# Attention and MLP backward for one token: all DMAs off GpSimd's queue, and the last head in another order

## Chip, cores and metric

The kernel runs on 1 core of a Trainium2 chip. The metric is the device time in microseconds, the median of several executions.

## The reference

One decode token goes through an attention block with a cache (A) and a Mish MLP (B), mixed by a gate; the result and the gradients for the token, both caches, all weights and the gate are wanted.

```python
def _A_ref(x, k_cache, v_cache, wq, wo):          # H=32 heads, Sk=4096, Dh=128, D=640
    q = (x @ wq).reshape(B, Sq, H, Dh).transpose(0, 2, 1, 3)
    scores = einsum("bhqd,bhkd->bhqk", q, k_cache) * (Dh ** -0.5)
    p = softmax(scores)
    o = einsum("bhqk,bhkd->bhqd", p, v_cache)
    return o.transpose(0, 2, 1, 3).reshape(B, Sq, H * Dh) @ wo

def _B_ref(x, w1, b1, w2):                        # F=1728
    h = einsum("bsd,df->bsf", x, w1) + b1
    act = h * tanh(softplus(h))
    return einsum("bsf,fd->bsd", act, w2)

g = sigmoid((x * gate_w).sum(-1, keepdims=True))
out = g * _A_ref(A_x, ...) + (1 - g) * _B_ref(B_x, ...)
# outputs: out, and its gradients by A_x, k_cache, v_cache, wq, wo, w1, b1, w2, gate_w
```

Everything is bf16. Each head reads K and V (1 MB each) and writes dK and dV (1 MB each): 128 MB of the 165 MB that are moved.

## The kernel before

**Tiles.** K and V of a head are [128, 32, 128]: partition p holds 32 consecutive rows, 8 KB of them. The 32 heads come in 8 groups of G = 4. A group has its 512 columns of wq as `wq_g` [128, 5, 512] (rows of 1,024 bytes in memory) and its rows of wo as `wo_g` [128, 4, 640] (rows of 1,280 bytes), 640 KB each, in rings of three. Their gradients dwq and dwo are written over them in place and stored from there. K has four buffers, V three, the outgoing `o_sb` tiles of dK and dV four. w1, w2 and their gradients live in `w1_sb` and `w2_sb`, 2.2 MB each.

**A head (loop at L581).** TensorE transposes V (`v_tr`) in four blocks of 8, each copied from PSUM by ScalarE (`tr_block`, L406 and L407). `softmax` takes the scores that were made a head earlier; `dP` multiplies the transposed V with the gradient of o; `zd_mm` sums over partitions; `probs` makes p and ds on VectorE. `dv_out` and `dk_out` are outer products on VectorE (L469, two halves), stored by SP (L480, L482). `k_tr` and `scores` prepare the next head, `dq_o` (L492) sums dq and o from K, V, ds and p, and then SP issues the loads of K for head h + 4 and V for head h + 3. dK of a head is made in the next head, except for the last.

**A group.** `g_do`, `g_qcol`, `g_q` and others prepare the next group's q and do rows from its wq and wo. After a group, `f_diag` and `f_bc` broadcast its dq; `f_aT_pe` multiplies o with wo (TensorE); `f_dx` multiplies wq with the broadcast dq on VectorE and sums along the row (the gradient of x); `f_dwq` (VectorE) and `f_dwo` (ScalarE) write the weight gradients; `f_dwq_st` and `f_dwo_st` store them. These run in the heads hh = 0 and hh = 1 of the next group.

**The MLP** is cut into pieces, taken by `mlp_some` and `dw2_some` at the end of each head as far as a budget goes. `m_h` makes a piece of h on one partition and a small DMA carries it over to 32 partitions; two such rows are in use at a time. By head 28 all pieces are done, and dw1 and dw2 are stored (L676 to L681). An engine takes its instructions in the written order, but GpSimd has so few that it runs ahead and issues these stores as soon as their data is there.

**Queues.** SP issues K, V, dK, dV, the MLP's weights, and wq and wo of groups 1 and 2. GpSimd (POOL) issues the other wq and wo loads (L131, L132, L654, L655), b1 (L149), the h rows (L308), dwq and dwo (L278, L284), dw1 and dw2 (L677 to L680) and one small result (L725). A queue's instructions wait in order: one that waits for a semaphore holds back all that stand behind it.

**The end (from L683).** For the last head, groups of its work are done for three heads inside the loop and for the fourth after it; then aT, dx and the gate's gradient are put together, transposed and stored.

Of the kernel before, what the change touches and what calls it, by code (L numbers as in the profile page):

```python
# [16 lines left out]
def kernel(  # L17
# [96 lines left out]
    def load_wq(g, eng):  # L114
        wqs[g] = wts.tile([P, RC, GD], BF16, name="wq_g", tag="wq_g")
        eng.dma_start(wqs[g][:], wq_v[:, :, g * GD:(g + 1) * GD])
# [11 lines left out]
    kts[0] = kv_in.tile([P, J, Dh], BF16, name="Kn", tag="Kn")  # L128
    for c in range(2):
        nc.sync.dma_start(kts[0][:, c * JH:(c + 1) * JH, :], Kv[0][:, c * JH:(c + 1) * JH, :])  # L130
    load_wq(0, nc.gpsimd)  # L131
    load_wo(0, nc.gpsimd)  # L132
    load_v(0)
    load_k(1)
    load_v(1)
# [10 lines left out]
    nc.sync.dma_start(w2_sb[0:FT, FR, :], B_w2[FM:F, :])  # L146
    b1_sb = const.tile([P, FCN], BF16, name="b1_sb")
    nc.vector.memset(b1_sb[:], 0.0)
    nc.gpsimd.dma_start(b1_sb[:, 0:FR], b1_v)  # L149
    nc.gpsimd.dma_start(b1_sb[0:FT, FR:FCN], b1_t)  # L150

    ident_bf = const.tile([P, P], BF16, name="ident_bf")
    nc.gpsimd.memset(ident_bf[:], 0.0)
# [111 lines left out]
    def f_dx(g, c, a=0, b=G, slot=None):  # L265
# [4 lines left out]
        nc.vector.scalar_tensor_tensor(junk[:, cs], in0=wqs[g][:, c, cs], scalar=1.0, in1=gp["dq_bc"][:, cs],  # L270
                                       op0=ALU.mult, op1=ALU.mult, accum_out=dx_parts[:, c, slot:slot + 1])

    def f_dwq(g, c, a=0, b=G):
        cs = slice(a * Dh, b * Dh)
        nc.vector.tensor_scalar(wqs[g][:, c, cs], groups[g]["dq_bc"][:, cs], x_col_f[:, c:c + 1], None, ALU.mult)  # L275

    def f_dwq_st(g):
        nc.gpsimd.dma_start(dwq_v[:, :, g * GD:(g + 1) * GD], wqs.pop(g)[:])  # L278

    def f_dwo(g, hh):  # L280
        nc.scalar.activation(wos[g][:, hh, :], da_bc[:], ACT.Copy, scale=groups[g]["dqo"][:, 1, hh:hh + 1])  # L281

    def f_dwo_st(g, a=0, b=G):
        nc.gpsimd.dma_start(dwo_v[:, g * G + a:g * G + b, :], wos[g][:, a:b, :])  # L284

    h_sb = const.tile([P, FCN], F32, name="h_sb")
    u_sb = const.tile([P, FCN], F32, name="u_sb")
# [11 lines left out]
    def m_h(i):  # L299
        n = FW if i < 4 else FT  # L300
        ps = grp([1, FW], F32, "h_ps")
        for rc in range(RC):
            nc.tensor.matmul(ps[:, 0:n], lhsT=x_col_bf[:, rc:rc + 1], rhs=w1_sb[:, rc, i * FW:i * FW + n],
                             start=(rc == 0), stop=(rc == RC - 1))
        row = dh_bc[0:1, :].bitcast(F32)[:, (i % 2) * FW:(i % 2) * FW + n]
        nc.scalar.copy(row, ps[:, 0:n])
        if i < 4:
            nc.gpsimd.dma_start(h_sb[i * P // 4:(i + 1) * P // 4, 0:FR], row)  # L308
        else:
            nc.gpsimd.dma_start(h_sb[0:FT, FR:FCN], row)  # L310

    def m_np(fc):
        return P if fc < FR else FT
# [264 lines left out]
    g_q(0)  # L578
    g_qs(0)

    for h in range(H):  # L581
        g, hh = h // G, h % G
        nx, pv, last = g + 1 < NG, g > 0, h == H - 1
        v_tr(h, 0)
        v_tr(h, 1)
        mx = softmax(h)
        if h > 0:
            dk_out(h - 1)
        if last:
            f_new(g)  # L590
            f_diag(g, 0, 3)
        if hh == 0 and pv:
            g_dobc(g)
        v_tr(h, 2)
        v_tr(h, 3)
        dP(h)
        if hh == 0 and pv:
            f_bc(g - 1)
            f_aT_pe(g - 1)
        if last:  # L600
            f_bc(g, 0, 3)
            f_aT_pe(g, 0, 3)
        k_tr(h + 1, 0)
        k_tr(h + 1, 1)
        zd_mm(h, mx)
        if hh == 0 and pv:
            f_dx(g - 1, 0)
        if hh == 1 and pv:
            f_dx(g - 1, 3)
        if hh == 2 and nx:  # L610
            g_do(g + 1, 0)
        if hh == 3 and nx:
            g_do(g + 1, 3)
        probs(h, mx)
        k_tr(h + 1, 2)
        k_tr(h + 1, 3)
        dv_out(h)
        scores(h + 1)
        od = dq_o(h)
        load_k(h + KBUFS)  # L620
        load_v(h + VBUFS)
        if last:
            dk_out(h)
        dqo_red(h, od)
        budget = 0.0
        if last:
            for i in range(3):
                f_dwo(g, i)
            f_dwo_st(g, 0, 3)
            for c in range(RC):  # L630
                f_dx(g, c, 0, 3)
            for c in range(RC):
                f_dwq(g, c, 0, 3)
        if hh == 0:
            if nx:
                g_new(g + 1)
            if pv:
                f_aT_add(g - 1)
                f_dx(g - 1, 1)
                f_dx(g - 1, 2)  # L640
                f_dwo(g - 1, 0)
                f_dwo(g - 1, 1)
            budget = 2.7
        if hh == 1:
            if pv:
                f_dx(g - 1, 4)
                for c in range(RC):
                    f_dwq(g - 1, c)
                f_dwq_st(g - 1)
                f_dwo(g - 1, 2)  # L650
                f_dwo(g - 1, 3)
                f_dwo_st(g - 1)
            if g + 2 < NG:
                load_wq(g + 2, nc.gpsimd if pv else nc.sync)  # L654
                load_wo(g + 2, nc.gpsimd if pv else nc.sync)  # L655
            budget = 1.8
        if hh == 2:
            if nx:
                g_do(g + 1, 1)
                g_do(g + 1, 2)  # L660
                g_qcol(g + 1)
            budget = 2.7
        if hh == 3:
            if nx:
                g_docol(g + 1)
                g_dodiag(g + 1)
                g_q(g + 1)
                g_qs(g + 1)
                f_new(g)
                f_diag(g)  # L670
            budget = 1.8
        if h >= 2:
            mlp_some(budget)
            dw2_some(2)
        if h == H - 4:
            assert not mq and dw2_next[0] == FCN  # L676
            nc.gpsimd.dma_start(dw1_v, w1_sb[:])  # L677
            for a, b in W2P:
                nc.gpsimd.dma_start(dw2_v[:, a:b, :], w2_sb[:, a:b, :])
            nc.gpsimd.dma_start(out_8[FM:F, :], w2_sb[0:FT, FR, :])  # L680
            nc.sync.dma_start(db1_row, dh_bc[0:1, :])  # L681

    g = NG - 1  # L683
    f_diag(g, 3, 4)
    f_aT_add(g)
    f_bc(g, 3, 4)
    f_aT_pe(g, 3, 4)
    f_dwo(g, 3)
    f_dwo_st(g, 3, 4)
    for c in range(RC):  # L690
        f_dx(g, c, 3, 4, NG)
    for c in range(RC):
        f_dwq(g, c, 3, 4)
    f_dwq_st(g)
    f_aT_add(g)

    fin = const.tile([P, 3 * RC], F32, name="fin")
    gb = const.tile([P, RC], F32, name="gb")
    nc.vector.tensor_scalar(gb[:], bT[:], omg_all[:], None, ALU.mult)
    nc.vector.scalar_tensor_tensor(fin[:, 0:RC], in0=aT_acc[:], scalar=g_all[:], in1=gb[:], op0=ALU.mult, op1=ALU.add)  # L700
    amb = const.tile([P, RC], F32, name="amb")
    nc.vector.tensor_tensor(amb[:], aT_acc[:], bT[:], ALU.subtract)
# [3 lines left out]
                                   accum_out=dgp[:])  # L706
    dg_ps = grp([P, 1], F32, "dg_ps")
    nc.tensor.matmul(dg_ps[:], lhsT=ones_f[:], rhs=dgp[:], start=True, stop=True)
    gg = const.tile([P, 1], F32, name="gg")
    nc.vector.tensor_tensor(gg[:], g_all[:], omg_all[:], ALU.mult)  # L710
    dz = const.tile([P, 1], F32, name="dz")
    nc.vector.tensor_tensor(dz[:], dg_ps[:], gg[:], ALU.mult)
    nc.vector.tensor_scalar(fin[:, 2 * RC:3 * RC], x_col_f, dz[:], None, ALU.mult)
    dxs = const.tile([P, RC], F32, name="dxs")
    nc.vector.reduce_sum(dxs[:], dx_parts[:], axis=AX.X)
# [6 lines left out]
    fin_rows = const.tile([3 * RC, P], BF16, name="fin_rows")  # L722
    nc.scalar.copy(fin_rows[:], fin_ps[:])
    nc.scalar.dma_start(out0_rows, fin_rows[0:RC, :])
    nc.gpsimd.dma_start(out1_rows, fin_rows[RC:2 * RC, :])  # L725
    nc.sync.dma_start(out9_rows, fin_rows[2 * RC:3 * RC, :])


# [28 lines left out]
```

## Time and profile before

| | us |
|---|---|
| median of 3 runs | 419.07 (418.73 to 420.15) |
| profiled execution, its own time | 423.44 |
| its span, first to last instruction | 421.7 |
| TensorE busy | 318.5 (76%) |
| VectorE busy | 307.6 (73%) |
| ScalarE busy | 212.8 (50%) |
| GpSimd busy | 38.1 (9%) |

A page of the profile has the busy time of each engine, the span in 40 slices of 10.5 us (busy tenths, the granted TensorE clock, the busy share of the 16 DMA engines and the GB/s they moved), the DMA queues, the chain of work that ended last, the costliest groups of instructions, and the DMA issues with the time to their landing. PE is TensorE, DVE VectorE, ACT ScalarE, POOL GpSimd; L406 is line 406. Two groups and four kinds of issue that matter here:

```profile
L469 DVE TENSOR_TENSOR o_sb<-qs_row,ds 128x2048 bf16<-128x2048 bf16 x64 | 78.1, 1260 | 6.4 <-DMA out_dram<-o_sb 6.4
...
L270 DVE SCALAR_TENSOR_TENSOR junk<-wq_g,dq_bc 128x512 bf16<-128x512 bf16 (+2 forms) x45 | 27.1, 627 | 4.4 <-ACT dq_bc L233 4.4
...
out_dram<-wq_g POOLq DMA_DIRECT2D x8, 640.0 KB, 10.5
out_dram<-wo_g POOLq DMA_DIRECT2D x7, 640.0 KB, 14.1
wq_g<-in_A_wq_dram POOLq DMA_DIRECT2D x6, 640.0 KB, 11.8
wo_g<-in_A_wo_dram POOLq DMA_DIRECT2D x6, 640.0 KB, 12.2
```

The trace behind the page can be asked for any stretch: the instructions in order of time with what ended the wait before them, the chain of waits, the landing of each DMA, and sums by window.

### The profile page before, as it was taken

The numbers are of one execution on the slowest core, as the hardware profiler recorded it, in microseconds if no ns is written. First come the engines' busy times: TensorE is split into PE (matmuls) and PEld (weight loads), VectorE is DVE, ScalarE is ACT, GpSimd is POOL, SyncE is SP. The second block draws the span as 40 slices with busy tenths as digits, with TensorE's granted clock in tenths as the row PEclk, the third lists the DMA queues.
The fourth block names the chain that finished last, engine by engine and source line by source line (L and its number), as shares of the span: only waits on it lengthen the run. The fifth ranks groups of instructions, "written<-read, shape, count | busy, mean of one in ns | idle before, by whom it ended". The sixth has DMA issues, their size and how long they took to land.

```text
span 421.7 us, 15327 instructions
## 1 busy us (share of the span) xinstructions
PE 318.5 (76%) x6749; PEld 288.9 (69%) x6757; DVE 307.6 (73%) x837; ACT 212.8 (50%) x439; POOL 38.1 (9%) x61
## 2 busy tenths in 40 slices
PE   1598949878689779877987797877778888657621
PEld 1487928778679778767877686876768776647620
DVE  0536735788859987799979788689887975728683
ACT  2255425674346544655577765655346644436321
POOL 5000010001100100001104100001100310001001
PEclk9999888999699898898997989688898998869955
DMA  8999999999999999999999999999999999999783
GB/s 301 390 410 421 422 399 416 392 364 410 412 400 393 378 421 404 423 420 380 418 401 424 419 420 408 420 401 368 418 396 411 390 419 409 415 421 390 308 332 112
DMA packets 28073, 165.05 MB, mean 391 GB/s; under 512 B 3092, under 2 KB 5461, under 8 KB 12006
## 3 DMA queue, kind: packets, MB, share of 16 engines
q1 hardware_dynamic: 22412, 141.28, 83.0%
q0 software_dynamic: 5552, 22.79, 13.7%
q8 instruction: 53, 0.87, 0.8%
q14 instruction: 14, 0.11, 0.1%
q10 hardware_dynamic: 42, 0.01, 0.0%
HBM read 82.03 MB, written 82.03 MB: 389 GB/s over the span
## 4 chain that ended last, share of the span: by engine, by line
PE 33%; issue 21%; ACT 19%; DVE 17%; DMA 6%; POOL 1%; POOLq 0%; ACTq 0%; DVEq 0%
PE tr L406 14%; PE od L492 9%; ACT VT L407 8%; ACT KT L407 6%; DMA wo_g<-in_A_wo_dram 3%; DVE o_sb L469 3%; PE S L412 3%; DVE junk L366 2%; PE DP L412 2%; DVE junk L219 2%; PE q_ps L197 2%; DVE mjunk L388 2%; ACT e_bf L443 2%; DMA out_dram<-o_sb 2%; DMA h_sb<-dh_bc 2%
## 5 line engine op out<-in xcount | busy, mean ns | idle before, releaser
L406 PE MATMUL tr<-ident_bf,Vn 128*128 128x128 bf16 x1024 | 76.6, 232 | 28.7 <-ACT VT L407 18.6
L407 ACT COPY KT<-tr 128x512 f32<-128x512 f32 x128 | 70.7, 587 | 50.9 <-PE tr L406 50.7
L406 PEld LDWEIGHTS <-Vn 128*128 128x128 bf16 x1024 | 68.4, 105 | 38.7 <-issue 28.5
L406 PE MATMUL tr<-ident_bf,Kn 128*128 128x128 bf16 x1024 | 84.5, 247 | 7.7 <-DMA Kn<-in_A_k_cache_dram 5.0
L406 PEld LDWEIGHTS <-Kn 128*128 128x128 bf16 x1024 | 77.7, 115 | 9.8 <-DMA Kn<-in_A_k_cache_dram 5.0
L469 DVE TENSOR_TENSOR o_sb<-qs_row,ds 128x2048 bf16<-128x2048 bf16 x64 | 78.1, 1260 | 6.4 <-DMA out_dram<-o_sb 6.4
L407 ACT COPY VT<-tr 128x512 f32<-128x512 f32 x128 | 69.1, 586 | 22.3 <-PE tr L406 21.9
L469 DVE TENSOR_TENSOR o_sb<-do_row,p 128x2048 bf16<-128x2048 bf16 x64 | 75.2, 1217 | 1.2 <-DMA out_dram<-o_sb 1.2
L412 PE MATMUL DP<-doz,VT 128*128 128x32 bf16 x1024 | 39.6, 179 | 24.9 <-ACT VT L407 21.5
L412 PEld LDWEIGHTS <-VT 128*128 128x128 bf16 x1024 | 33.0, 97 | 29.9 <-ACT VT L407 29.4
L412 PE MATMUL S<-qz,KT 128*128 128x32 bf16 x1024 | 37.1, 180 | 3.0 <-ACT KT L407 0.4
L434 ACT ACTIVATE dgm<-ident_bf,m 128x128 f32<-128x128 bf16 x32 | 12.8, 402 | 50.8 <-DVE m L432 50.8
L412 PEld LDWEIGHTS <-KT 128*128 128x128 bf16 x1024 | 32.5, 98 | 6.3 <-ACT KT L407 5.5
L492 PE MATMUL od<-p,Vn 128*128 128x32 bf16 x1024 | 31.6, 177 | 3.9 <-issue 3.9
L492 PE MATMUL od<-ds,Kn 128*128 128x32 bf16 x1024 | 31.2, 178 | 2.6 <-issue 1.5
L492 PEld LDWEIGHTS <-Vn 128*128 128x128 bf16 x1024 | 28.5, 96 | 4.4 <-issue 4.4
L492 PEld LDWEIGHTS <-Kn 128*128 128x128 bf16 x1024 | 28.7, 97 | 2.8 <-issue 2.8
L270 DVE SCALAR_TENSOR_TENSOR junk<-wq_g,dq_bc 128x512 bf16<-128x512 bf16 (+2 forms) x45 | 27.1, 627 | 4.4 <-ACT dq_bc L233 4.4
L219 DVE SCALAR_TENSOR_TENSOR junk<-wo_g,da_bc 128x640 bf16<-128x640 bf16 x32 | 25.4, 819 | 0.4 <-DMA wo_g<-in_A_wo_dram 0.4
L278 POOL DMA_DIRECT2D out_dram<-wq_g x8 | 7.1, 884 | 206.3 <-DVE wq_g L275 106.2
L281 ACT ACTIVATE wo_g<-da_bc,dqo 128x640 bf16<-128x640 bf16 x32 | 24.5, 814 | 0.0
L440 DVE TENSOR_REDUCE negM<-mx 128x1 f32<-128x128 f32 x32 | 9.2, 286 | 20.2 <-PE mx L438 20.2
(146 smaller groups left out, 319.4 us busy)
## 6 DMA issues: line engine op xcount, KB each, us to landing
out_dram<-o_sb SPq DMA_DIRECT2D x62, 1024.0 KB, 12.2
Vn<-in_A_v_cache_dram SPq DMA_DIRECT2D x32, 1024.0 KB, 14.8
Kn<-in_A_k_cache_dram SPq DMA_DIRECT2D x31, 1024.0 KB, 15.2
out_dram<-wq_g POOLq DMA_DIRECT2D x8, 640.0 KB, 10.5
out_dram<-wo_g POOLq DMA_DIRECT2D x7, 640.0 KB, 14.1
wq_g<-in_A_wq_dram POOLq DMA_DIRECT2D x6, 640.0 KB, 11.8
wo_g<-in_A_wo_dram POOLq DMA_DIRECT2D x6, 640.0 KB, 12.2
w_sb<-in_B_w_dram SPq DMA_DIRECT2D x1, 2160.0 KB, 17.1
```

The source lines that it names most:

```text
L197: nc.tensor.matmul(ps[:], lhsT=x_col_bf[:, rc:rc + 1].to_broadcast([P, P]), rhs=wqs[g][:, rc, :], start=(rc == 0), stop=(rc == RC - 1))
L219: nc.vector.scalar_tensor_tensor(junk[:], in0=wos[g][:, hh, :], scalar=1.0, in1=da_bc[:], op0=ALU.mult, op1=ALU.mult, accum_out=gp["do_col ...
L270: nc.vector.scalar_tensor_tensor(junk[:, cs], in0=wqs[g][:, c, cs], scalar=1.0, in1=gp["dq_bc"][:, cs], op0=ALU.mult, op1=ALU.mult, accum_ ...
L281: nc.scalar.activation(wos[g][:, hh, :], da_bc[:], ACT.Copy, scale=groups[g]["dqo"][:, 1, hh:hh + 1])
L366: nc.vector.scalar_tensor_tensor(junk[0:n, :], in0=w2_sb[0:n, fc, :], scalar=dm[0:n, fc:fc + 1], in1=db_bc[0:n, :], op0=ALU.mult, op1=ALU. ...
L406: nc.tensor.transpose(tp[:, t, :], src[:, c * TB + t, :], ident_bf[:])
L407: nc.scalar.copy(dst[:, sl, :].rearrange("p a b -> p (a b)").bitcast(F32), tp[:].rearrange("p a b -> p (a b)").bitcast(F32))
L412: nc.tensor.matmul(out, lhsT=T[:, j, :], rhs=zrow[:, J - 1 - j:2 * J - 1 - j], start=(j == 0), stop=(j == J - 1))
L434: nc.scalar.activation(dgms[h][:], ident_bf[:], ACT.Copy, scale=m32[:])
L440: nc.vector.tensor_reduce(negM[:], mx[:, 0:P], axis=AX.X, op=ALU.max, negate=True)
L469: nc.vector.tensor_tensor(dst[:, a:b, :].rearrange("p j (k t) -> p j k t", t=4), row.rearrange("p (k t) -> p k t", t=4).unsqueeze(1).to_br ...
L492: nc.tensor.matmul(out, lhsT=N[:, j, :], rhs=c4[:, 4 * j:4 * j + W], start=(j == 0), stop=(j == J - 1))
```

## The change

Three things change.

- **Queues.** wq and wo of group 0, b1, the h rows and all dwo stores are issued by ScalarE; the later wq and wo loads and the dwq stores by SP; the MLP's gradients by SP, dw2 at the end of head 28 and dw1 at the end of head 29, behind the last V load. GpSimd issues no DMA.
- **Places in the loop.** A group's dwq store stands at the end of head hh = 2 (before: hh = 1), the load of wq and wo two groups ahead at the end of hh = 3 (before: hh = 1).
- **The last head** leaves the loop and is written out. Its wq group is transposed (20 blocks, `wq_tr`), into a free K buffer, and `l_pe` makes both aT and dx of the last group by TensorE, for three heads first and then for the fourth; `f_dx` is not used there. `l_dwq` makes the fourth head's dwq on ScalarE. dK of head 30 comes after `probs` of head 31, and dV and dK of head 31 come last, after the sums of the small results.

```diff
-    load_wq(0, nc.gpsimd)
-    load_wo(0, nc.gpsimd)
+    load_wq(0, nc.scalar)
+    load_wo(0, nc.scalar)
...
-    nc.gpsimd.dma_start(b1_sb[:, 0:FR], b1_v)
+    nc.scalar.dma_start(b1_sb[:, 0:FR], b1_v)
...
+    def wq_tr(k):
+        if k == 0:
+            wqT[0] = kv_in.tile([P, J, Dh], BF16, name="Kn", tag="Kn")
+        n = min(TB, G * RC - k * TB)
+        tp = tr_ps.tile([P, TB, P], BF16, name="tr", tag="tr")
+        for t in range(n):
+            hh, c = divmod(k * TB + t, RC)
+            nc.tensor.transpose(tp[:, t, :], wqs[NG - 1][:, c, hh * Dh:(hh + 1) * Dh], ident_bf[:])
+        nc.scalar.copy(wqT[0][:, k * TB:k * TB + n, :].rearrange("p a b -> p (a b)").bitcast(F32),
+                       tp[:, 0:n, :].rearrange("p a b -> p (a b)").bitcast(F32))
...
+    def l_dqbf(a, b):
+        gp = groups[NG - 1]
+        nc.vector.tensor_scalar(gp["dq_bf"][:, a:b], gp["dqo"][:, 0, a:b], scale, None, ALU.mult)
+
+    def l_pe(a, b):
+        gp = groups[NG - 1]
+        gp["ax"] = grp([P, 2, RC], F32, "ax_ps")
+        for i in range(2):
+            for c in range(RC):
+                for hh in range(a, b):
+                    nc.tensor.matmul(gp["ax"][:, i, c:c + 1],
+                                     lhsT=wqT[0][:, hh * RC + c, :] if i else wos[NG - 1][:, hh, c * P:(c + 1) * P],
+                                     rhs=gp["dq_bf" if i else "o_bf"][:, hh:hh + 1],
+                                     start=(hh == a), stop=(hh == b - 1))
+
+    def l_add(slot):
+        ax = groups[NG - 1]["ax"]
+        nc.vector.tensor_tensor(aT_acc[:], aT_acc[:], ax[:, 0, :], ALU.add)
+        nc.vector.tensor_copy(dx_parts[:, :, slot], ax[:, 1, :])
+
+    def l_dwq(c, a, b):
+        cs = slice(a * Dh, b * Dh)
+        nc.scalar.activation(wqs[NG - 1][:, c, cs], groups[NG - 1]["dq_bc"][:, cs], ACT.Copy,
+                             scale=x_col_f[:, c:c + 1])
...
     def f_dwq_st(g):
-        nc.gpsimd.dma_start(dwq_v[:, :, g * GD:(g + 1) * GD], wqs.pop(g)[:])
+        nc.sync.dma_start(dwq_v[:, :, g * GD:(g + 1) * GD], wqs.pop(g)[:])
...
     def f_dwo_st(g, a=0, b=G):
-        nc.gpsimd.dma_start(dwo_v[:, g * G + a:g * G + b, :], wos[g][:, a:b, :])
+        nc.scalar.dma_start(dwo_v[:, g * G + a:g * G + b, :], wos[g][:, a:b, :])
...
-            nc.gpsimd.dma_start(h_sb[i * P // 4:(i + 1) * P // 4, 0:FR], row)
+            nc.scalar.dma_start(h_sb[i * P // 4:(i + 1) * P // 4, 0:FR], row)
...
-    for h in range(H):
+    for h in range(H - 1):
...
-                f_dwq_st(g - 1)
                 f_dwo(g - 1, 2)
                 f_dwo(g - 1, 3)
                 f_dwo_st(g - 1)
-            if g + 2 < NG:
-                load_wq(g + 2, nc.gpsimd if pv else nc.sync)
-                load_wo(g + 2, nc.gpsimd if pv else nc.sync)
             budget = 1.8
         if hh == 2:
+            if pv:
+                f_dwq_st(g - 1)
...
         if hh == 3:
+            if g + 2 < NG:
+                load_wq(g + 2, nc.sync)
+                load_wo(g + 2, nc.sync)
...
         if h == H - 4:
-            nc.gpsimd.dma_start(dw1_v, w1_sb[:])
             for a, b in W2P:
-                nc.gpsimd.dma_start(dw2_v[:, a:b, :], w2_sb[:, a:b, :])
-            nc.gpsimd.dma_start(out_8[FM:F, :], w2_sb[0:FT, FR, :])
+                nc.sync.dma_start(dw2_v[:, a:b, :], w2_sb[:, a:b, :])
+            nc.sync.dma_start(out_8[FM:F, :], w2_sb[0:FT, FR, :])
+        if h == H - 3:
+            nc.sync.dma_start(dw1_v, w1_sb[:])
             nc.sync.dma_start(db1_row, dh_bc[0:1, :])
...
+    v_tr(h, 0)
+    v_tr(h, 1)
+    mx = softmax(h)
+    f_new(g)
+    l_new()
+    f_diag(g, 0, 3)
+    l_dqbf(0, 3)
+    v_tr(h, 2)
+    v_tr(h, 3)
+    dP(h)
+    zd_mm(h, mx)
+    f_bc(g, 0, 3)
+    for k in range(3):
+        wq_tr(k)
+    l_pe(0, 3)
+    probs(h, mx)
+    dk_out(h - 1)
+    od = dq_o(h)
+    l_add(g)
+    for i in range(3):
+        f_dwo(g, i)
+    f_dwo_st(g, 0, 3)
+    dqo_red(h, od)
     f_diag(g, 3, 4)
-    f_aT_add(g)
+    l_dqbf(3, 4)
     f_bc(g, 3, 4)
-    f_aT_pe(g, 3, 4)
+    l_pe(3, 4)
+    for c in range(RC):
+        f_dwq(g, c, 0, 3)
+    for c in range(RC):
+        l_dwq(c, 3, 4)
+    f_dwq_st(g)
     f_dwo(g, 3)
     f_dwo_st(g, 3, 4)
-    for c in range(RC):
-        f_dx(g, c, 3, 4, NG)
-    for c in range(RC):
-        f_dwq(g, c, 3, 4)
-    f_dwq_st(g)
-    f_aT_add(g)
+    l_add(NG)
...
     nc.tensor.matmul(dg_ps[:], lhsT=ones_f[:], rhs=dgp[:], start=True, stop=True)
+    dv_out(h)
...
     nc.scalar.dma_start(out0_rows, fin_rows[0:RC, :])
-    nc.gpsimd.dma_start(out1_rows, fin_rows[RC:2 * RC, :])
-    nc.sync.dma_start(out9_rows, fin_rows[2 * RC:3 * RC, :])
+    nc.sync.dma_start(out1_rows, fin_rows[RC:2 * RC, :])
+    nc.scalar.dma_start(out9_rows, fin_rows[2 * RC:3 * RC, :])
+    dk_out(h)
```

More of the change, by code (lines that the diff above doesn't have):

```diff
@@ L148 @@
     nc.vector.memset(b1_sb[:], 0.0)
-    nc.gpsimd.dma_start(b1_sb[:, 0:FR], b1_v)
-    nc.gpsimd.dma_start(b1_sb[0:FT, FR:FCN], b1_t)
+    nc.scalar.dma_start(b1_sb[:, 0:FR], b1_v)
+    nc.scalar.dma_start(b1_sb[0:FT, FR:FCN], b1_t)
     ident_bf = const.tile([P, P], BF16, name="ident_bf")
@@ L271, in f_dx, with l_new @@
                                        op0=ALU.mult, op1=ALU.mult, accum_out=dx_parts[:, c, slot:slot + 1])
+    wqT = {}
+    def wq_tr(k):
[8 more added lines that the diff above has]
+                       tp[:, 0:n, :].rearrange("p a b -> p (a b)").bitcast(F32))
+    def l_new():
+        gp = groups[NG - 1]
+        gp["dq_bf"] = grp_sb.tile([P, G], BF16, name="dq_bf", tag="dq_bf", bufs=1)
+    def l_dqbf(a, b):
+        gp = groups[NG - 1]
+        nc.vector.tensor_scalar(gp["dq_bf"][:, a:b], gp["dqo"][:, 0, a:b], scale, None, ALU.mult)
+    def l_pe(a, b):
+        gp = groups[NG - 1]
+        gp["ax"] = grp([P, 2, RC], F32, "ax_ps")
[14 more added lines that the diff above has]
+                             scale=x_col_f[:, c:c + 1])
     def f_dwq(g, c, a=0, b=G):
@@ L307, in m_h @@
         if i < 4:
-            nc.gpsimd.dma_start(h_sb[i * P // 4:(i + 1) * P // 4, 0:FR], row)
+            nc.scalar.dma_start(h_sb[i * P // 4:(i + 1) * P // 4, 0:FR], row)
         else:
-            nc.gpsimd.dma_start(h_sb[0:FT, FR:FCN], row)
+            nc.scalar.dma_start(h_sb[0:FT, FR:FCN], row)
     def m_np(fc):
@@ L579 @@
     g_qs(0)
-    for h in range(H):
+    for h in range(H - 1):
         g, hh = h // G, h % G
-        nx, pv, last = g + 1 < NG, g > 0, h == H - 1
+        nx, pv = g + 1 < NG, g > 0
         v_tr(h, 0)
@@ L588 @@
             dk_out(h - 1)
-        if last:
-            f_new(g)
-            f_diag(g, 0, 3)
         if hh == 0 and pv:
@@ L599 @@
             f_aT_pe(g - 1)
-        if last:
-            f_bc(g, 0, 3)
-            f_aT_pe(g, 0, 3)
         k_tr(h + 1, 0)
@@ L621 @@
         load_v(h + VBUFS)
-        if last:
-            dk_out(h)
         dqo_red(h, od)
         budget = 0.0
[L626 to L629, printed above, removed]
-            for c in range(RC):
-                f_dx(g, c, 0, 3)
-            for c in range(RC):
-                f_dwq(g, c, 0, 3)
         if hh == 0:
@@ L676 @@
             assert not mq and dw2_next[0] == FCN
-            nc.gpsimd.dma_start(dw1_v, w1_sb[:])
             for a, b in W2P:
-                nc.gpsimd.dma_start(dw2_v[:, a:b, :], w2_sb[:, a:b, :])
-            nc.gpsimd.dma_start(out_8[FM:F, :], w2_sb[0:FT, FR, :])
+                nc.sync.dma_start(dw2_v[:, a:b, :], w2_sb[:, a:b, :])
+            nc.sync.dma_start(out_8[FM:F, :], w2_sb[0:FT, FR, :])
+        if h == H - 3:
+            nc.sync.dma_start(dw1_v, w1_sb[:])
             nc.sync.dma_start(db1_row, dh_bc[0:1, :])
-    g = NG - 1
+    g, h = NG - 1, H - 1
+    gb = const.tile([P, RC], F32, name="gb")
+    nc.vector.tensor_scalar(gb[:], bT[:], omg_all[:], None, ALU.mult)
+    gg = const.tile([P, 1], F32, name="gg")
+    nc.vector.tensor_tensor(gg[:], g_all[:], omg_all[:], ALU.mult)
+    v_tr(h, 0)
[21 more added lines that the diff above has]
+    dqo_red(h, od)
     f_diag(g, 3, 4)
-    f_aT_add(g)
+    l_dqbf(3, 4)
     f_bc(g, 3, 4)
-    f_aT_pe(g, 3, 4)
+    l_pe(3, 4)
[4 more added lines that the diff above has]
+    f_dwq_st(g)
     f_dwo(g, 3)
     f_dwo_st(g, 3, 4)
-    for c in range(RC):
-        f_dx(g, c, 3, 4, NG)
-    for c in range(RC):
-        f_dwq(g, c, 3, 4)
-    f_dwq_st(g)
-    f_aT_add(g)
+    l_add(NG)
     fin = const.tile([P, 3 * RC], F32, name="fin")
-    gb = const.tile([P, RC], F32, name="gb")
-    nc.vector.tensor_scalar(gb[:], bT[:], omg_all[:], None, ALU.mult)
     nc.vector.scalar_tensor_tensor(fin[:, 0:RC], in0=aT_acc[:], scalar=g_all[:], in1=gb[:], op0=ALU.mult, op1=ALU.add)
@@ L708 @@
     nc.tensor.matmul(dg_ps[:], lhsT=ones_f[:], rhs=dgp[:], start=True, stop=True)
-    gg = const.tile([P, 1], F32, name="gg")
-    nc.vector.tensor_tensor(gg[:], g_all[:], omg_all[:], ALU.mult)
+    dv_out(h)
+    dxs = const.tile([P, RC], F32, name="dxs")
+    nc.vector.reduce_sum(dxs[:], dx_parts[:], axis=AX.X)
     dz = const.tile([P, 1], F32, name="dz")
@@ L713 @@
     nc.vector.tensor_scalar(fin[:, 2 * RC:3 * RC], x_col_f, dz[:], None, ALU.mult)
-    dxs = const.tile([P, RC], F32, name="dxs")
-    nc.vector.reduce_sum(dxs[:], dx_parts[:], axis=AX.X)
     nc.vector.scalar_tensor_tensor(fin[:, RC:2 * RC], in0=gw_col_f, scalar=dz[:], in1=dxs[:], op0=ALU.mult,
```

## The prediction

> **What bounds the kernel now.** I read the page's slices and queue lines first, then the chain of waits at the start, then the time order of TensorE and the windows at the end.
>
> ```profile
> span 421.7 us, 15327 instructions
> ...
> DMA  8999999999999999999999999999999999999783
> GB/s 301 390 410 421 422 399 416 392 364 410 412 400 393 378 421 404 423 420 380 418 401 424 419 420 408 420 401 368 418 396 411 390 419 409 415 421 390 308 332 112
> DMA packets 28073, 165.05 MB, mean 391 GB/s; under 512 B 3092, under 2 KB 5461, under 8 KB 12006
> ...
> q1 hardware_dynamic: 22412, 141.28, 83.0%
> q0 software_dynamic: 5552, 22.79, 13.7%
> ```
>
> The DMA engines are busy in every slice but the first and the last three, yet the best slices move 420 to 424 GB/s and others 364 to 390. The middle is therefore not at the limit of the DMA all the time. Engines rarely wait for data there: TensorE waited for a V load twice, 7.7 us in all, both times after 370 us. Between 40 and 350 us the chain goes transpose, ScalarE copy, product, VectorE and round again, at 9 to 15 us a head. So compute paces the middle, with the DMA close behind; the ends can be won or lost.
>
> The queue lines hold a second thing. POOL's queue (q0) averages 22.79 MB / 5552 = 4.1 KB a packet, although its wq and wo transfers are made of rows of 1,024 and 1,280 bytes: four rows go into one packet. SP's queue does not do this. It has 5461 - 3092 = 2369 packets of 512 B to 2 KB, and wq1, wq2, wo1, wo2 on SP have 2 x 640 + 2 x 512 = 2304 rows (the last w2 piece has 64, dy 1). One row, one packet.
>
> The chain of waits from 0 to 30 us:
>
> ```profile
> 1.28 1.04 POOL wq_g L116
> 2.32 14.07 DMA wo_g<-in_A_wo_dram
> 16.39 0.03 issue
> ```
>
> The first head starts when the first wo group has landed, at 16.39 us; wq landed at 12.1 (TensorE's first L209 product, 12.14). The chain from 50 to 63 us has one more DMA in it:
>
> ```profile
> 53.52 0.50 ACT dh_bc L306
> ...
> 54.64 6.50 DMA h_sb<-dh_bc
> ```
>
> The third row of the MLP's h cannot be written before the first has been carried off. The end, by time on TensorE and by windows (busy by engine, then granted clock, DMA share, GB/s):
>
> ```profile
> 366.48 0.96 PE L492 MATMUL od<-p,Vn 128*128 128x32 bf16 x32
> 374.03 1.89 PE L406 MATMUL tr<-ident_bf,Vn 128*128 128x128 bf16 x16 [6.59 <-DMA Vn<-in_A_v_cache_dram]
> ```
>
> ```profile
> 385.00:395.00 10.00, 9.01 (x213) 8.46 (x214) 7.20 (x17) 5.76 (x13) 1.70 (x2) 1.00 0.95 377
> 395.00:405.00 10.00, 5.62 (x134) 4.82 (x132) 6.11 (x15) 4.80 (x10) 0.73 (x1) 0.78 0.59 242
> 405.00:422.00 17.00, 1.30 (x12) 0.91 (x9) 10.20 (x49) 1.25 (x3) 2.02 (x4) 0.50 0.55 208
> ```
>
> V of head 29 is 6.6 us late; then the last head leaves the DMA idle for 0.5 + 4.1 + 7.6 = 12.2 us of the last 37. Head 31 begins at 394.0 (its V transposes), so it and the end take 421.7 - 394.0 = 27.7 us.
>
> All sums are made against this execution: span 421.7, its own time 423.44, the median of the runs 419.07. I carry a difference in span over to the median unchanged.
>
> **The start: wq0 and wo0 from ScalarE, +7.** ScalarE issues them after its four small loads, at about 2.3 and 2.7 us (those took 0.27 to 0.56 each), POOL did at 1.28 and 2.32. The issue is no loss; the share is. By the packet records from 6 to 11 us, POOL's 4,096-byte packets and SP's 8,192-byte ones come about one for one (35 and 34 from 8 to 9 us). If ScalarE's queue takes turns likewise, but with one row a packet, each of its 49 ns rows waits for one of SP's 321 ns packets. Per DMA engine wq0 has 640/16 = 40 rows; SP's queue holds some 31 large packets ahead of its own short rows (rest of V0, K1, V1, K2): 31 x 0.37 + 9 x 0.1 = 12.4 us. From 6 us, where POOL's first packets were, wq0 lands near 19.3 instead of 12.1. wo0 follows against SP's wq1 and wo1 rows, 32 x 0.11 = 3.5, at 22.8. VectorE's products with wo0 came 4.3 us after wq0, so at 23.6 instead of 16.5: +7. The other end: shares by bytes bring both in by 11 us, and the chain starts 4 earlier. Range -4 to +7.5; I take +7, since both queues' packet sizes are counted above.
>
> [...]
>
> **Shorter packets elsewhere, +2.** Moved to SP or ScalarE are 14 transfers of wq's form (6 loads, 8 stores) and 14 of wo's (6 loads, 8 stores' worth). By the packet records, 640 rows x 49.1 ns replace 160 packets x 168.6 ns: 4.4 us over 16 engines, 0.28 each; 512 x 60.6 replace 128 x 203.5: 0.31 each. Sum 14 x 0.59 = 8.2 us of DMA time, 12,100 more packets. Windows agree in kind: 370 GB/s at 56 to 60 us, when wq2 and wo2 move in rows, 427 right after. A group of four heads moves 4 x 4.19 + 2.62 = 19.4 MB, 46.2 us at 420 GB/s, 47.3 with rows; groups take about 48 (POOL's dwq stores at 94.9, 143.1, 191.5, 236.9, 287.0, 333.9). It nearly fits: I take +2, bounds 0 and +8.2.
>
> [...]
>
> **Queues and waits in the loop, +1.** On SP, the dwq store goes in a head after its VectorE work, so it waits for nothing. The next wq load, a head later, reuses its slot and waits until the store has landed (10.5 us median now, a head is 9 to 13); at most some 3 us, behind which only a K or V store is queued, with four output slots in hand; the group is needed three heads later. ScalarE issues dwo stores and h rows itself: 0.3 to 0.5 us each, at seven places next to the V copies, covered where VectorE is later: +1 (0 to +3). POOL's 0.5 to 0.9 us issues vanish from an engine that bounds nothing.
>
> **h rows, -2.6.** From the row's end (54.02) to landing (61.15) is 7.1 us. From ScalarE it lies between 2.4 (SP's wait for the last row stores on an empty queue) and 7.1; I take 4.5.
>
> **MLP gradients after the last V load, -8.** POOL issues 4.4 MB of dw1 and dw2 at 335.5 to 338; they share the DMA with V29 and V30 until 376 (26 us median to land). On SP they stand behind V31. The waits of 6.59 and 1.14 us at 374.0 and 385.0 go; of VectorE's waits for output slots (7.6 us, five times) a little goes too, the rest lies beside them. Heads 28 to 30 then pace themselves by compute, 30 to 31 us as heads 24 to 26 did, instead of 38.7. Bounds 0 and -13. What is late next is the stores: dw1, dw2 fill the DMA until about 395.
>
> **The last head, -3.5.** Removed from VectorE: ten dx products (5 x 0.55 + 5 x 0.28 = about 4.1 us with their accumulator reads) and five 128-wide dwq (0.9, now ScalarE, about 1.5 beside it). Added: 20 transposes (about 2 us at the low clock) and three ScalarE copies (1.5), 40 one-column products (15 took 0.58, so 1.6), small adds 0.6. From the V transposes: dP ends +4.3, probabilities +6.0, dK of head 30 +8.3. TensorE meanwhile: +4.9, broadcast 0.5, transposes 2.0, products 1.2, dq and o 2.0: +10.6. VectorE again: dqo and diagonals +11.3, dwq +12.5, sums +13.4, dV +15.7, the small results +16.7, dK +19.1. Its last half megabyte lands 1.3 (bytes at 391 GB/s) + 2.4 later, and the end needs 1.4 more (420.31 to 421.7): 24.2, against 27.7. Bounds -6 and +1. The small result stores change queues at no cost: three issues of 0.3 us beside the 2.35 us of dK.
>
> **Sum:** +7 + 2 + 1 - 2.6 - 8 - 3.5 = -4.1: span 417.6, median 415.0. The DMA agrees: 165.05 MB at the 408 GB/s of the middle is 404.5 us, and with 8.2 of rows, 2.3 at the start and 1.4 at the end, 416.4.
>
> **Rivals.** *ScalarE's queue gets a fair share:* start -4 instead of +7, span 406 to 408, median 404 to 407 with DMA catching up at 408. For it: nothing on the page shows two hardware queues with heavy loads. Against: one row, one packet. Chance 0.12. *The rows decide (slower):* if the middle has no slack, its 8.2 us stay and the DMA bounds all. Of 12.2 us idle at the end, about 5.1 must stay for the last landing and drain: -7.1 + 8.2 = +1.1, and +1 to +3 when the late start lets the 15.6 MB of prefetch run out near 41 us: 424 to 426, median 421 to 423. It decides from 6 us of the 8.2 on. For it: DMA share of 1.00 from 20 to 385 us. Against: groups at 45.4 us (191.5 to 236.9). Chance 0.28. *The change does not do what it says:* the deferred 4.4 MB only moves the idle time, the start costs 7 and the ends win the same: 418 to 420. Chance 0.15. *My forecast:* 0.45.
>
> **Numbers.** 415.0. About 0.3% (1.3 us) is what can be told from no change. Faster 0.57 (forecast and fair share), same 0.15, slower 0.28. The likeliest case's own range is 411 to 418; for 8 in 10 I reach from 407 to 423.
>
> **What would show it.** q0 all but gone; some 40,000 packets; wq0 landing near 19 us and wo0 near 23; no V wait near 374; head 31's transposes near 393; after them about 24 us with dK last. Wrong if the first L209 product comes at or before 12 us, if the groups grow beyond 49 us, or if SP's wait for a landed dwq store holds up K and V loads.

## The result: 5% slower, and the profile after

The changed kernel takes **440.87 us** (439.08 to 442.37), the kernel before in the same job 419.61 (418.73 to 421.32): ratio **1.0487**, 95% interval 1.0454 to 1.052. The forecast was 415.0 with a range up to 423, so direction and size are both wrong. A ratio leaves out executions more than 1.5% above the fastest of the same kernel, which touches one version below only (wq and wo loads and dwq stores on SP alone: four of twelve left out).

The page after, the lines that answer to those shown of before:

```profile
span 439.4 us, 15362 instructions
...
DMA  8999978998999969999999999999699999999978
GB/s 305 352 407 418 409 287 279 333 397 327 335 409 402 419 241 383 412 402 418 347 407 415 404 394 387 414 401 418 245 388 415 399 415 366 418 416 414 418 274 335
DMA packets 40786, 165.05 MB, mean 376 GB/s; under 512 B 3342, under 2 KB 21903, under 8 KB 24720
...
q1 hardware_dynamic: 34748, 157.50, 90.9%
q10 hardware_dynamic: 5972, 6.57, 4.2%
```

The same 165.05 MB move at 376 GB/s in place of 391. The best slices reach 415 to 419 (before: 420 to 424), but the middle now has holes: 287 and 279 between 55 and 77 us, then 241, 347, 245 and others. The forecast looked for time at the start, in the rows and at the end; the holes are elsewhere. What SP, which issues K, V, dK and dV, waited for in the changed kernel (line, what ended the wait, total us, times, longest):

```profile
SPq L107 <- DMA out_dram<-wo_g: 90.1, 6, 17.1
...
SPq L116 <- DMA out_dram<-wq_g: 27.5, 5, 7.0
...
SPq L524 <- DMA h_sb<-dh_bc: 11.2, 1, 11.2
...
SPq L116 <- DMA wq_g<-in_A_wq_dram: 10.7, 1, 10.7
```

L107 is the load of K. It waits six times, 15 us each, for a dwo store. The two have no tile in common, and the store is not SP's: ScalarE issues it. One of the six, by SP's issues in order of time and by two windows (busy by engine, then clock, DMA share, GB/s), with the second window of the kernel before below them:

```profile
97.25 0.34 SPq L524 DMA_DIRECT2D out_dram<-o_sb  x1
109.25 0.34 SPq L107 DMA_DIRECT2D Kn<-in_A_k_cache_dram  x1
109.68 0.38 SPq L112 DMA_DIRECT2D Vn<-in_A_v_cache_dram  x1
```

```profile
102.00:106.00 4.00, 3.78 (x92) 3.62 (x93) 3.68 (x11) 2.17 (x5) 0.00 (x0) 1.00 1.00 405
106.00:110.00 4.00, 3.56 (x99) 3.29 (x96) 2.93 (x11) 1.43 (x3) 0.00 (x0) 1.00 0.44 164
```

```profile
106.00:110.00 4.00, 1.63 (x28) 1.52 (x26) 3.49 (x21) 0.00 (x0) 0.86 (x1) 0.86 1.00 416
```

ScalarE issued that dwo store at 99.22. SP issues nothing from 97.6 to 109.25; what is queued drains, and from 106 to 110 the DMA moves 164 GB/s in place of 416.

**Why a load waits for a stranger's store.** The records of the two traces name for each transfer the semaphore that tells of its landing. In the changed kernel the 165 transfers of SP and the 24 of ScalarE share eight semaphores, 23 or 24 transfers on each; the eight, taken in turn, fit the order of both engines from the first transfer to the last. Of the 181 transfers after the first eight, 166 carry a wait for their own semaphore. In the kernel before, 142 transfers of SP and 5 of ScalarE share eight in the same way (139 of 139 carry the wait), and the 42 of GpSimd have eight others. The kernel's text names none of this. Each of the six K loads stands eight places behind a dwo store of ScalarE, on the same semaphore, and goes out less than 0.1 us after the last of the 16 marks that the store leaves on it:

| dwo store issued by ScalarE, us | semaphore | its last mark, us | issue to last mark, us | K load issued by SP, us |
|---|---|---|---|---|
| 99.22 | 105 | 109.18 | 10.0 | 109.25 |
| 147.27 | 100 | 162.31 | 15.0 | 162.38 |
| 194.82 | 105 | 211.15 | 16.3 | 211.22 |
| 244.08 | 100 | 260.09 | 16.0 | 260.15 |
| 297.05 | 105 | 312.49 | 15.4 | 312.56 |
| 344.93 | 100 | 361.27 | 16.3 | 361.34 |

In the kernel before, where SP has the turn nearly to itself, this costs little: the transfer eight places back is an older one of its own queue, and the longest of SP's waits for a landing is 4.6 us. With ScalarE in the same turn, SP waits for a transfer that ScalarE issues late, after computing, and that then lands late. SP issues four or five transfers a head (dV, dK, K, V, now and then a weight), so eight places are less than two heads of 9 to 15 us, and a store that ScalarE reaches late and that then takes 10.0 to 16.3 us to land is not through by then.

What SP has behind the held load waits with it: V goes at 109.68, right behind K, and the DMA share falls to 0.44 from 106 to 110 us.

### The profile page after: what moved, and what is told of

Read it like the earlier page. It is cut to its first block, busy times and chain, and to the rows that moved or that the text cites. A ratio compares the mean times of both kernels' runs of the same rounds, so it can differ in the third digit from the quotient of the medians.

```text
span 439.4 us, 15362 instructions
## 1 busy us (share of the span) xinstructions
PE 320.2 (73%) x6797; PEld 288.5 (66%) x6797; DVE 300.8 (68%) x816; ACT 216.3 (49%) x447; POOL 7.0 (2%) x19
## 2 busy tenths in 40 slices
DMA packets 40786, 165.05 MB, mean 376 GB/s; under 512 B 3342, under 2 KB 21903, under 8 KB 24720
## 4 chain that ended last, share of the span: by engine, by line
DMA 44%; PE 24%; ACT 13%; DVE 12%; issue 3%; ACTq 1%; DVEq 0%; SPq 0%
DMA out_dram<-o_sb 22%; DMA Vn<-in_A_v_cache_dram 18%; PE tr L448 10%; ACT VT L449 6%; PE od L534 6%; ACT KT L449 4%; DMA wq_g<-in_A_wq_dram 4%; DVE o_sb L511 2%; PE S L454 2%; PE DP L454 2%; DVE mjunk L430 2%; DVE junk L219 2%; PE q_ps L197 1%; ACT e_bf L485 1%; DMA h_sb<-dh_bc 1%
## 5 line engine op out<-in xcount | busy, mean ns | idle before, releaser
L511 DVE TENSOR_TENSOR o_sb<-qs_row,ds 128x2048 bf16<-128x2048 bf16 x64 | 75.5, 1222 | 27.7 <-DMA out_dram<-o_sb 27.7
L448 PE MATMUL tr<-ident_bf,Vn 128*128 128x128 bf16 x1024 | 74.7, 229 | 26.7 <-ACT VT L449 16.5
L448 PEld LDWEIGHTS <-Vn 128*128 128x128 bf16 x1024 | 66.5, 103 | 39.5 <-issue 25.0
L454 PEld LDWEIGHTS <-VT 128*128 128x128 bf16 x1024 | 33.0, 97 | 28.6 <-ACT VT L449 27.7
L534 PEld LDWEIGHTS <-Vn 128*128 128x128 bf16 x1024 | 28.5, 96 | 3.4 <-issue 3.4
L270 DVE SCALAR_TENSOR_TENSOR junk<-wq_g,dq_bc 128x512 bf16<-128x512 bf16 x35 | 23.5, 686 | 2.5 <-ACT dq_bc L233 2.5
L496 PE MATMUL mx<-zd,ones_f 128*128 128x2 f32 x64 | 13.1, 274 | 13.0 <-DVE pj L492 12.9
```

The lines of the kernel that those rows point to most:

```text
L448: nc.tensor.transpose(tp[:, t, :], src[:, c * TB + t, :], ident_bf[:])
L454: nc.tensor.matmul(out, lhsT=T[:, j, :], rhs=zrow[:, J - 1 - j:2 * J - 1 - j], start=(j == 0), stop=(j == J - 1))
L496: nc.tensor.matmul(mx[:, P:P + 2], lhsT=ones_f[:], rhs=zds[h][:], start=True, stop=True)
L511: nc.vector.tensor_tensor(dst[:, a:b, :].rearrange("p j (k t) -> p j k t", t=4), row.rearrange("p (k t) -> p k t", t=4).unsqueeze(1).to_br ...
L534: nc.tensor.matmul(out, lhsT=N[:, j, :], rhs=c4[:, 4 * j:4 * j + W], start=(j == 0), stop=(j == J - 1))
```

## The experiments

The theory is the one above: **ScalarE's transfers hold up SP**, through the shared semaphores. The rivals: the short rows cost by their own DMA time (the forecast's rival *the rows decide*); the late start; the new order of the last head.

### Taking the dwo stores off ScalarE

Two kernels, each the changed kernel with one word replaced:

```diff
-        nc.scalar.dma_start(dwo_v[:, g * G + a:g * G + b, :], wos[g][:, a:b, :])
+        nc.gpsimd.dma_start(dwo_v[:, g * G + a:g * G + b, :], wos[g][:, a:b, :])
```

and in the second kernel `nc.sync` in that place.

> The changed kernel with the dwo stores back on POOL's queue, all else as changed. Theory (SP stands still because its K loads wait for a completion semaphore that a dwo store of ScalarE's slow queue holds): SP's waits for dwo (90.1 us in the loop, 11.7 at the end) are gone, the DMA no longer idles at 106-110 and 158-163 us, and the last stores are issued some 12 us earlier: 421 to 425 us. Rival (the short rows cost the DMA): only half of the rows are gone, 436 to 438. Rival (the late start): unchanged, 441.

> The changed kernel with the dwo stores on SP's queue, at the same places: no DMA on POOL, all rows stay short, but ScalarE's queue holds nothing in the loop but the h rows. Theory (semaphore held by a slow queue): 422 to 427, 1 to 2 above e1 for SP's wait for ScalarE's dwo. Rival (short rows): no gain, 440. This run and e1 together tell the queue from the rows.

GpSimd: 429.47 us, ratio to before 1.0223 (1.0183 to 1.0264). SP: 428.81, 1.0214 (1.0179 to 1.0249). Both win back about 12 of the 21 us. GpSimd sends the rows in longer packets (37,715 in all), SP one by one (40,787), and the times are the same within some 2 us: a cost of the dwo rows themselves does not show. The issuing engine does. Both kept more loss than expected, so something else costs too.

### One part alone on the kernel before

The last head alone (all queues as before):

> The kernel before with the new last head alone, all queues and places as before. My forecast's term of -3.5 stands: 415 to 417. Rival (the new order of the last head is what costs, because the last two stores of 1 MB come last): 424 to 430.

419.3 us, 0.9978 (0.9945 to 1.001): no measurable gain, and no part of the loss.

The start alone:

```diff
-    load_wq(0, nc.gpsimd)
-    load_wo(0, nc.gpsimd)
+    load_wq(0, nc.scalar)
+    load_wo(0, nc.scalar)
```

> The kernel before with wq and wo of group 0 issued by ScalarE, nothing else. Theory (one row a packet, turns one for one): wq0 lands near 18 us instead of 12, the first dV store is some 5 us later than 32.0, and the time is 422 to 426 if nothing later makes it good. Rival (later waits absorb a late start): 419 to 420.

427.15 us, 1.0176 (1.0124 to 1.0227): +7.4, kept to the end. wq0 landed at 19.46 us, VectorE's products with wo0 began at 23.50 (16.49 before) and the first store of dV went at 38.70 (32.04 before). SP stood here too, 11.5 us for wq0, but the DMA share from 10 to 20 us stayed above 1.00, so that hold left no idle time there.

The MLP gradients late on SP's queue, alone and together with the last head:

> The kernel before with one part of the change: the gradients of W1 and W2 go by SyncE's queue, W2's behind the loads of head 28's pass and W1's behind head 29's, in place of GpSimd's queue at 335 us. Everything else stands as before. By the forecast's own term (V of head 30 no longer waits near 374 us, bounds 0 to -13): 419.5 - 8 = 411 to 412. Rival, the tail is set by the sum of bytes and no wait goes that isn't replaced by the late stores at the end: 418 to 421, with SyncE held behind the gradient stores near 375 to 390 us. My own guess after the first four runs: a gain of 3 to 6, 414 to 417, since the stores that are put off now lie where the last heads' dV and dK stores want to be.

> The kernel before with two parts of the change: the new last head, and the MLP gradients late on SyncE's queue. All other transfers where they were. By the forecast's terms: 419.5 - 3.5 - 8 = 408. If the parts add as measured (the last head alone gave -0.9) with a gain of 3 to 6 for the gradients: 413 to 416. Rival, the late gradient stores collide with the last head's stores at the end: 418 to 422.

Alone 419.02 us, 0.9976 (0.9953 to 0.9999): -1.0. Together 417.74, 0.9949 (0.9923 to 0.9974): -2.1, the fastest version of all. The waits for V after 370 us are gone in both, and head 31 begins 12 us earlier. The kernel with the gradients alone, TensorE in order of time and two windows at the end:

```profile
381.84 1.05 PE L406 MATMUL tr<-ident_bf,Vn 128*128 128x128 bf16 x16
```

```profile
385.00:395.00 10.00, 2.56 (x63) 2.15 (x60) 4.31 (x13) 2.84 (x6) 0.00 (x0) 0.71 1.03 422
395.00:405.00 10.00, 1.56 (x59) 1.46 (x55) 6.76 (x16) 0.48 (x1) 0.77 (x1) 0.50 0.93 381
```

From there the end takes 415.3 - 381.8 = 33.5 us in place of 27.7, as the rival had it: the DMA, idle for 4.1 us between 395 and 405 before, is full (1.03 and 0.93), and TensorE is nearly idle beside it (2.56 and 1.56 of 10). The 4.4 MB were not saved but moved to where the last stores want to go.

The h rows alone on ScalarE (five stores, 7 KB in all, in packets of 52 and 4 bytes: 128 and 64 of them, not the 80 that GpSimd makes of the same rows):

```diff
-            nc.gpsimd.dma_start(h_sb[i * P // 4:(i + 1) * P // 4, 0:FR], row)
+            nc.scalar.dma_start(h_sb[i * P // 4:(i + 1) * P // 4, 0:FR], row)
```

> The kernel before with the five h rows issued by ScalarE and nothing else. They are 80 packets of 52 or 104 bytes, so no theory of bandwidth or turns sees them. By the forecast's term: -2.6, 417. By the theory that SyncE's and ScalarE's transfers share a few completion semaphores in turn, so that a K load of SyncE's waits until an h row that ScalarE issued late has landed: the K load that was issued at 67.38 in the run with the dwo stores on GpSimd stood still until the h row issued at 63.61 landed at 67.32, with the queue empty from 60 to 64; here the same hold, SyncE waiting 3 to 15 us for h_sb near 60 to 68 us, and 422 to 425. Rival, the rows matter to nobody: 419 to 420.

426.99 us, 1.016 (1.0136 to 1.0184): **+6.7 for 7 KB**. SP's waits, and its issues in order of time:

```profile
SPq L482 <- DMA h_sb<-dh_bc: 14.1, 2, 10.1
SPq L120 <- DMA h_sb<-dh_bc: 11.5, 1, 11.5
```

```profile
48.01 0.38 SPq L116 DMA_DIRECT2D wq_g<-in_A_wq_dram  x1
59.95 0.38 SPq L120 DMA_DIRECT2D wo_g<-in_A_wo_dram  x1
64.37 0.84 SPq L482 DMA_DIRECT2D out_dram<-o_sb  x2
```

The load of wo stands still for 11.5 us until an h row has landed; the dK store behind it goes at 64.37, when the h row issued at 60.0 lands (4.3 us to landing, so 64.3). What that leaves to the DMA (share and GB/s at the end of the lines):

```profile
57.00:60.00 3.00, 0.33 (x3) 0.16 (x3) 2.56 (x3) 0.49 (x1) 0.00 (x0) 0.89 0.32 103
60.00:62.00 2.00, 0.78 (x8) 0.78 (x8) 0.00 (x0) 1.36 (x5) 0.00 (x0) 0.50 0.40 64
```

The same windows before moved 372 and 432 GB/s.

The loads of wq and wo and the dwq stores alone on SP, at the changed places (those lines of the diff and nothing else):

> The kernel before with the loads of wq and wo from group 3 on and the dwq stores taken from GpSimd's queue to SyncE's, at the changed kernel's places; dwo stores, h rows, start and end as before. This is the terms 'shorter packets elsewhere' (+2, bounds 0 to 8) without the dwo rows, and 'queues and waits in the loop' (+1) without ScalarE: forecast 420.5 to 423. By the theory of the shared completion semaphores SyncE holds itself up only behind its own wq store and the landing of it, a few us in all: 421 to 424. Rival, rows of 1,024 and 1,280 bytes alone decide: 425 or more. Rival, nothing: 419 to 420.

425.78 us in the middle of a wide spread (420.11 to 429.24), ratio 1.0078 (1.0042 to 1.0115): +3.3 by the ratio, +5.8 by the medians of all executions. The first lies where the shared semaphores put it (421 to 424 us), the second where the rival of the short rows did (425 or more), so this run does not part the two. SP waits for its own dwq store before the next wq load:

```profile
SPq L116 <- DMA out_dram<-wq_g: 23.6, 5, 7.3
```

The dwo stores alone on ScalarE:

> The kernel before with the dwo stores alone issued by ScalarE (rows of 1,280 bytes) and all else as it was. The changed kernel gained 11.4 and 12 when these stores were taken off ScalarE. If the parts add, 419.5 + 11.5 = 431; what the other parts leave of the measured loss of 21 (start 7.4, h rows 6.7, wq places 3.3, tail -2.1) is 5.7, so 425 if the parts cover each other otherwise. Semaphore theory: SyncE's K load behind each dwo store stands until it lands, at seven places. Rival, the short rows cost by their bytes alone: 421.

428.57 us, 1.0204 (1.0171 to 1.0238): +8.6. Here a store of dK waits, not a load of K, six times and 104.5 us in all: which of SP's transfers is hit is not the same in the two kernels. SP's wait row and the issues around one such place:

```profile
SPq L482 <- DMA out_dram<-wo_g: 104.5, 6, 20.8
```

```profile
91.38 1.03 SPq L112 DMA_DIRECT2D Vn<-in_A_v_cache_dram  x1
105.38 0.82 SPq L482 DMA_DIRECT2D out_dram<-o_sb  x2
```

ScalarE issued this dwo store at 91.4; it took 13.9 us to land, at 105.3, and SP goes on at 105.38.

### A transfer that nobody needs

The rows of h stay on GpSimd; ScalarE gets five loads of 52 bytes that nothing reads:

```diff
+    pads = [const.tile([1, 26], BF16, name=f"pad{i}") for i in range(5)]
...
             nc.gpsimd.dma_start(h_sb[0:FT, FR:FCN], row)
+        nc.scalar.dma_start(pads[i][:], dy_row[:, 0:26])
```

> The kernel before, with the h rows on GpSimd as they were, and five loads added that nothing reads: 52 bytes each, one packet, issued by ScalarE just behind the copy of each h row, where the last experiment but two had ScalarE issue the row itself. By the theory of the completion semaphores shared in turn by SyncE's and ScalarE's transfers, the transfer of SyncE's that stands eight places behind such a load waits until it has landed, and the kernel loses as much as with the h rows on ScalarE: 425 to 428, SyncE held until near 60 and 64 us by a tile that it has nothing to do with. Rival, what costs time with the h rows is the way of the rows itself (ScalarE's issue, the MLP behind them): 419 to 421.

423.31 us, 1.0067 (1.0042 to 1.0091): +2.8, between the two numbers expected, but clearly not the rival's nothing. The holds are at the places named:

```profile
SPq L485 <- DMA pad<-in_grad_out_dram: 12.4, 2, 8.5
...
SPq L120 <- DMA pad<-in_grad_out_dram: 9.7, 1, 9.7
```

SP issues wo at 57.98 and the dK store at 62.38, both after a wait that a pad's landing ended; the pad before the second was issued by ScalarE at 59.0, some 3.4 us earlier. So 260 bytes without a reader hold SP for 22 us, and the kernel loses 2.8. The real h rows lost 6.7: they land 4.3 us after their issue, about 1 us later than a pad, and held the wo load and the store 2 us longer each. The DMA windows with the pads:

```profile
57.00:60.00 3.00, 0.00 (x0) 0.00 (x0) 2.34 (x3) 0.94 (x2) 0.27 (x1) 1.00 0.56 141
60.00:62.00 2.00, 1.74 (x41) 1.63 (x41) 0.00 (x0) 1.90 (x6) 0.22 (x1) 0.99 0.78 286
```

By the DMA shares from 57 to 66 us the DMA is idle for 2.9 us with the pads (0.56, 0.78, 0.47, 0.97), for 4.8 us with the h rows on ScalarE (0.32, 0.40, 0.74, 0.46) and not at all before. The losses, 2.8 and 6.7, go the same way; whether anything else belongs to the 6.7 was not tried.

### All of ScalarE's transfers back, and a start in one queue

The changed kernel with wq0, wo0, b1, the h rows and the dwo stores on GpSimd again:

> The changed kernel with all that ScalarE was given put back on GpSimd's queue: wq0, wo0, b1, the h rows and the dwo stores. What stays of the change: wq and wo loads, dwq stores and MLP gradients on SyncE's queue, and the new last head. Theory: the loss was ScalarE's transfers, so this stands at 419.5 + 3.3 (wq places, measured alone) - 2.1 (tail, measured alone) = 420.7, range 417 to 424. Rival, the loss comes from anything else in the change as well: 428 or more.

420.2 us, 1.0006 (0.9981 to 1.0031), against 420.7 expected. Without ScalarE's transfers nothing of the loss is left. The rest of the change, wq places +3.3 and tail -2.1 when alone, comes out even within the interval (-0.8 to +1.3 us); SP waits 13.2 us for its dwq stores here, 23.6 when the wq places are changed alone.

A better start, tried on the fastest version: wq0 and wo0 on SP's queue between K and V of head 0.

```diff
-    load_wq(0, nc.gpsimd)
-    load_wo(0, nc.gpsimd)
+    load_wq(0, nc.sync)
+    load_wo(0, nc.sync)
```

> The version with the new last head and the late MLP gradients, all else as before (measured 417.7), with wq0 and wo0 issued by SyncE directly behind K of head 0 and ahead of V of head 0, in one queue, so that no turns are taken. Before, wo0 landed at 16.4 and the chain of waits starts with it. In one queue: K0 landed at 6.3, then 640 rows of 1,024 bytes at 48.9 ns and 512 of 1,280 bytes at 58.8 ns over 16 engines, 2 + 1.9 us, so wo0 by about 10.5 to 11.5, and the first head begins when V of head 0 is there, near 13. Expected: the start 3 to 4 us earlier, of which the bytes let through 1 to 3: 414.5 to 417. Rival, the bytes of the whole kernel set the end and the start gains nothing, 417.5 to 419; or V of head 0 is late and it loses, 420.

418.31 us, 0.997 (0.9946 to 0.9994): no faster than the 417.74 without it. The start is indeed 4 us earlier; the first store of dV, 32.04 before:

```profile
28.04 0.35 SPq L524 DMA_DIRECT2D out_dram<-o_sb  x1
```

The lead lives until head 28 (its V transposes at 349.6, 354 without the new start) and is gone at head 31 (381 and 382). A lead is given back near the end, where the bytes decide; the lag that ScalarE's start caused was kept. The bytes tell the two apart: in the first 60 us the early start moved 23.20 MB and its base 23.27, while ScalarE's start moved 22.13 and the kernel before 23.31, which is 2.8 us at 420 GB/s.

## Why the prediction was wrong, point by point

Each part alone, against the kernel before (parts by the ratios, in brackets by the medians of all executions; the whole by the medians):

| part | forecast, us | measured, us |
|---|---|---|
| start: wq0, wo0 by ScalarE | +7 | +7.4 |
| h rows by ScalarE | -2.6 | +6.7 |
| dwo stores by ScalarE | in "loop" and "rows" | +8.6 |
| wq and wo loads, dwq stores on SP | in "loop" and "rows" | +3.3 (+5.8) |
| MLP gradients late | -8 | -1.0 |
| last head | -3.5 | -0.9 |
| the last two together | -11.5 | -2.1 |
| whole change | -4.1 | +21.3 |

The measured parts sum to 7.4 + 6.7 + 8.6 + 3.3 - 2.1 = 23.9. The whole is 21.3 by the medians, so the parts cover each other by a few us (by some 5 with +5.8 for the wq places).

- **The step that failed is "Queues and waits in the loop, +1".** It counted what ScalarE's issues cost ScalarE (0.3 to 0.5 us each) and asked what stands behind a waiting instruction on SP only for SP's own wq load. That a transfer of ScalarE's can be what SP waits for was not in it. The profile of before has a hint that I passed over: SP's load of K for head 2, whose buffer had never been used, waits until the first half of K of head 0, eight places back on the same semaphore, has landed (`SPq L107 <- DMA Kn<-in_A_k_cache_dram: 1.6, 1, 1.6`). (The next issue of K, from 7.04 to 17.72 us, is another matter: there the issuing instruction itself takes 10.68 us after its waits, and why is not shown.) The last sentence of "what would show it" came near, but named the wrong store: the dwq store's hold exists (27.5 us in five waits, 23.6 when alone, up to 7.3 each where I had allowed 3) and costs at most the few us of the wq places; the dwo store's hold is 90.1 us. So the step put at +1 what came to +8.6 for the dwo stores alone, and the same hold turned the h rows from -2.6 to +6.7. The second miss is the tail, -2.1 in place of -11.5: without ScalarE's transfers the change gives 420.2, no change, and not a gain.
- **h rows.** The landing came down, though by less than the 2.6 forecast: 3.9 us after the issue in the changed kernel where it is known, a median of 5.7 before; ScalarE's wait for a row went from 5.6 to 3.2. The price is SP's queue, which was not in the step.
- **Start.** Right in size. wq0 landed at 18.16 (forecast 19.3; the step's own terms, 6 + 12.4, give 18.4), VectorE's products with wo0 began at 22.19 (forecast 23.6; 23.50 with the start alone). One row a packet and turns one for one hold: from 9 to 16 us the packet records have 40 to 62 of ScalarE's 1,024-byte packets in each us beside 41 to 46 of SP's 8,192-byte ones. So this part of the loss comes from the turns and not, as far as the DMA shares tell (1.03 from 10 to 15 us, 0.94 from 15 to 20), from the shared semaphores. A part that I hadn't seen: SP stood until 18.18 for wq0's landing, the 10.7 us of the fourth row of waits above.
- **Shorter packets, +2.** 40,786 packets, as counted. The dwo rows show no cost between SP and GpSimd; the wq part is inside the +3.3, where it was not parted from SP's waits. The rival *the rows decide* is excluded as the cause: the version with no transfers on ScalarE keeps the wq and wo loads and the dwq stores in short rows (36,579 packets) and stands at 420.2.
- **MLP gradients.** The mechanism was right (the V waits go, head 31 begins 12 us earlier), the size was not. "What is late next is the stores" was written, but I charged nothing for it, although the sum of bytes that I made last, 416.4, is close to the measured end.
- **Last head.** -0.9 with an interval from -2.3 to +0.4: the 3.5 of compute are mostly not on the path, for the same reason.
- **The baseline.** The profiled execution of before, 423.44, lies near the top of the 29 that were run beside the second group of kernels (418.1 to 423.7, median 419.94). Terms read as a difference to its span of 421.7 were promised some 3 us too much: the fastest version's profile has a span of 416.0, 5.7 less, while its median is 2.1 less.
- **"Compute paces the middle"** was only half right. A lead of 4 us at the start was lost by the end and so was a lead of 12 us at head 31, while the holes that ScalarE's transfers made in the DMA stayed in the time.

## What to carry to other kernels

Before a transfer is moved to another queue, ask what the busy load queue will then wait for, and look for it in a trace. Here transfers that ScalarE issued late, and that landed late, held SP for 90.1 us in six waits (the dwo stores in the changed kernel); with the same stores on GpSimd, in the kernel before, none of SP's waits is for one. In a kernel whose DMA is busy in every slice, price a change by the DMA time that it leaves idle (2.9 and 4.8 us went with losses of 2.8 and 6.7), not by the waits of the compute engines: the 7.7 us of waits for V that were taken away near the end gave 1.0. Terms of 1 to 3 us need a baseline of several executions, not the span of one.

Issued on ScalarE, its transfers cost 20.7 us by the medians against the same kernel with them on GpSimd (440.87 and 420.2).

## What the runs showed of the hardware that I had not expected

- Five loads of 52 bytes with no reader, issued by ScalarE, cost the kernel 2.8 us; five stores of h rows, 7 KB together, 6.7 us. The size did not tell what a transfer held up: from 45 to 90 us SP waited 22.1 us for the pads and 28.2 for the h rows.
- A dwo store by ScalarE, 640 KB in rows of 1,280 bytes beside SP's packets of 8 KB, took 10.0 to 16.3 us to land in the changed kernel (the six that held K loads), 13.9 at the place shown where these stores alone were moved; GpSimd's in the kernel before, in packets of four rows, had a median of 14.1. Slow landing was there before; it held none of SP's transfers up.
- The dwo rows in 3,072 packets more (on SP, not on GpSimd) show no cost: 428.81 and 429.47 us.
